# Moving form stores to ScalarE's queue, scaling A11 ahead of four sums, and adding inside the last product

## The chip, the cores and the metric

The kernel runs on one core of a Trainium2 chip. The metric is the device time of one execution in microseconds; 727.01 us is the median of three runs before the change (725.63, 727.01 and 729.6). The engines named in the text are PE (TensorE: matrix products, results in eight PSUM banks of 128 x 512 f32), DVE (VectorE: elementwise sums and products), ACT (ScalarE: copies and activations), POOL (GpSimd, here little more than a source of DMA transfers) and SP (SyncE, only DMA transfers). Each engine works its own instructions strictly in the order in which the program lists them. An instruction whose input is not ready, or whose output place is still being read, waits, and everything behind it on the same engine waits with it. A DMA transfer is an instruction of the engine on whose queue it is issued.

## The reference

The input x is 2048 rows of 1024 (bf16). Two branches are computed from it and mixed row by row with a gate g:

```
g = sigmoid((x * gate_w).sum(-1))                    # one number per row
a = attention(x @ wqkv) @ wo                         # 32 heads, 8 keys per row at steps of 2
h = gelu(x @ w_gate) * (x @ w_up)                    # 2048 x 3584
out = g * a + (1 - g) * (h @ w_down)
```

The attention weights are multiplied by g and h by 1 - g before the last product, so that `out` is one product: [(1-g) h | g o] times [w_down ; wo], with o the attention's result. Its inner length is 3584 + 1024 = 4608, that is 36 tiles of 128, split into two halves of NK = 18 tiles.

## The kernel before

The kernel first computes the projections, the attention, and h and stores h and o to DRAM (h_d, o_d); this takes until about 515 us. What follows, and what the change touches, is `down(s)`: the last product, for s = 0 (rows 0 to 1023, "the first half") and s = 1 ("the second half", `last`).

**Strassen's scheme at two levels.** For each half, the left factor is a 2 x 2 set of blocks A11, A12, A21, A22 and the right factor R11 to R22, each block 128 x 18 x 512 in SBUF. Seven block products with sums of blocks in place of eight are formed; the sums of the right blocks, T1 to T4, were worked out earlier and lie in DRAM (t_d). S, S2 and AD are sums of left blocks. Most of the block products are made by `level2`, which does the same again one level lower: it cuts the blocks into quarters, and forms seven inner products of 18 matmuls of 128 x 256 each. It reads four "forms" of the left block (L1, L3 to L7, made by `forms_L`, four DVE sums) and of the right block (R1, R3 to R7, made by `forms_R`, of which the third is written in place over the quarter (0, 1) of the T block itself). Between the inner products, ACT copies partial results from one PSUM place to another (`then`, L1052); the fifth product's copies are the last. The result of inner product three is kept in SBUF (`part5`) and added to the right half of each bank afterwards by `join` (L1032, one for two banks; `joins` does both). Two sets of four banks, XT and VT, take turns, so that DVE and ACT empty one while PE fills the other. `zero_left` (L1025, ACT) clears the left halves of a set before `level2` accumulates in it.

**Buffers.** Ten buffers of 18 KB per partition hold all blocks and forms, by a fixed plan. A buffer that gets a new content must have been read by everyone who wants the old one. The entries that matter here: in the first half T1 and R6 and L4 share buffer 1, R5 and R7 buffer 5, R4 buffer 7, T4 buffer 9, T3 buffer 8; in the second half A21 takes buffer 9, A22 buffer 7, L1 buffer 5, R1 buffer 8, R21 buffer 1.

**Stores of forms.** The forms R5, R7 and R4 are needed in both halves and depend only on the weights. The first half stores them (`store_F`: the overwritten quarter of the T block to t_d, 576 KB in rows of 512 bytes, L991; three forms to r_d, 1,728 KB, L992), and the second half loads them (`load_F`). The stores are on POOL's queue, as are the first half's output stores (`emit`, L1077).

**Sums that give output.** `add_out` (L1081) adds a bank and an accumulator in SBUF (u2 or qs) into an output tile and stores it. There are six output tiles, used in turn; tiles 4 and 5 lie in the gate's memory (`omgrep`). The next user of a tile waits until its store has landed.

**The seam between the halves.** After the first half's last `level2` (on XT), DVE does two joins, four `add_out` of XT, then three scalings of A11 of the second half by 1 - g (`scale_task`, L916), and, between the four `add_out` of VT, the forms L1 and R1. PE meanwhile does the product A12 x R22 into VT (L1072) and then the second half's first `level2` (on XT), whose end is followed by joins, copies of XT into u2 (L1094) and further sums of PE into XT. Scalings of A12 and a first one of A21 stand on DVE ahead of those joins.

**The tail.** The second half's last `level2` (A12 x R22 into VT) is followed on DVE by two joins and eight half-width sums (`half_out`, L1191), and on SP by five output stores (L1193).

Of the kernel before, what the change touches and what calls it, by code (L numbers as in the profile page):

```python
# [9 lines left out]
ALU = mybir.AluOpType  # L10
# [5 lines left out]
P = 128  # L16
SC = 512
# [51 lines left out]
def kernel(  # L69
# [12 lines left out]
    nc = tc.nc  # L82
    Bsz, S, D = A_x.shape
# [3 lines left out]
    o2 = out.rearrange("b s d -> (b s) d")  # L87
# [36 lines left out]
    NE_ = NPAIR - 2  # L124
    h_d = [[tc.dram_tile([P, 4, k, SC], BF16, name=f"h_d{s}{e}") for e, k in enumerate((NE_, NPAIR - NE_))] for s in range(2)]
    o_d = [[tc.dram_tile([P, NT, SC], BF16, name=f"o_d{s}{c}") for c in range(2)] for s in range(2)]
    t_d = [tc.dram_tile([P, NK, SC], BF16, name=f"t_d{k}") for k in range(4)]
    r_d = {k: tc.dram_tile([P, 3 * (NK // 2) * (SC // 2)], BF16, name=f"r_d{k}") for k in (1, 3, 4)}
# [6 lines left out]
    TT = V.tensor_tensor  # L135

    with tc.manual_schedule(engines={mybir.EngineType.PE, mybir.EngineType.DVE, mybir.EngineType.Activation,
# [55 lines left out]
        def flat(a):  # L193
            return a.rearrange("p a b -> p (a b)")
# [689 lines left out]
        def tf_close():  # L884
            while tf_q[0] < N1:
# [8 lines left out]
                     T3=8, L7=4, R7=5, T4=9, L4=1, R4=7, R22=6),  # L894
# [3 lines left out]
        qs = regf(R_QS, 4 * SC).rearrange("p (j n) -> p j n", j=4)  # L898
        on = [0]

        def out_tile():
            k = on[0] % 6
            on[0] += 1
            return reg(R_OUT[k], SC) if k < 4 else omgrep[:, (k - 4) * SC:(k - 3) * SC]
# [3 lines left out]
        def Bs(s):  # L908
            return {k: bufs[v] for k, v in plan[s].items()}

        def scale_task(b, s, c, ia, ib):
            t0 = s * SUP + c * SC
            om = omgrep[:, t0:t0 + SC].rearrange("p (o s) -> p o s", o=1)
            for i0 in range(ia, ib, 4):
                i1 = min(i0 + 4, ib)
                TT(out=b[:, i0:i1, :], in0=b[:, i0:i1, :], in1=om.to_broadcast([P, i1 - i0, SC]), op=ALU.mult)  # L916
                yield 0.05 + 0.273 * (i1 - i0)
# [15 lines left out]
        def pieces(*gens):  # L933
            for g in gens:
                yield from g

        def take(g, k):
            for _ in range(k):
                if next(g, None) is None:
                    break  # L940
# [47 lines left out]
            nc.sync.dma_start(out=flat(rf)[:, 0:NF], in_=r_d[k][:])  # L988

        def store_F(rf, b, k):  # L990
            nc.gpsimd.dma_start(out=t_d[k - 1][:, 0:KH, HN:SC], in_=quarter(b, 0, 1))  # L991
            nc.gpsimd.dma_start(out=r_d[k][:], in_=flat(rf)[:, 0:NF])  # L992

        def quarter(b, kh, h):
            return b[:, kh * KH:(kh + 1) * KH, h * HN:(h + 1) * HN]
# [4 lines left out]
        def forms_L(f, b):  # L1000
            f = quads(f)
            q = lambda kh, h: quarter(b, kh, h)
            for o_, a, b_, op in ((f[:, 0], q(0, 1), q(1, 1), ALU.add), (f[:, 1], f[:, 0], q(0, 0), ALU.subtract),
                                  (f[:, 2], q(0, 0), q(0, 1), ALU.subtract), (f[:, 3], q(1, 0), f[:, 1], ALU.subtract)):
                TT(out=o_, in0=a, in1=b_, op=op)  # L1005
                yield 1.3

        def forms_R(f, b):
            f = quads(f)
            q = lambda kh, h: quarter(b, kh, h)  # L1010
            for o_, a, b_, op in ((f[:, 0], q(0, 1), q(0, 0), ALU.subtract), (f[:, 1], q(1, 1), f[:, 0], ALU.subtract),
                                  (q(0, 1), q(1, 1), q(0, 1), ALU.subtract), (f[:, 2], q(1, 0), f[:, 1], ALU.subtract)):
                TT(out=o_, in0=a, in1=b_, op=op)  # L1013
                yield 1.3

        def woven(*gens):
            for cs in zip(*gens):
                yield from cs
# [4 lines left out]
        def zero_left(bk):  # L1023
            for i in range(2):
                nc.scalar.activation(out=two_banks(bk, i, 0), in_=omgrep[:, SUP:SUP + SC].rearrange("p (a b) -> p a b", a=2),  # L1025
                                     func=ACT.Copy, scale=0.0)
# [4 lines left out]
        def join(bk, rf, i):  # L1031
            TT(out=two_banks(bk, i, 1), in0=two_banks(bk, i, 1), in1=part5(rf), op=ALU.add)  # L1032

        def joins(bk, rf):
            for i in range(2):
                join(bk, rf, i)

        def level2(bk, L, R, lf, rf, mid=None):
            p5d = part5(rf)
            lf, rf = quads(lf), quads(rf)  # L1040
            lq, rq = lambda r, c: quarter(L, c, r), lambda r, c: quarter(R, r, c)
            c = lambda i, h, j: banks[:, bk[2 * i + j], h * HN:(h + 1) * HN]

            def prod(i, h, l, r, then=None):
                for j in range(2):
                    for kt in range(KH):
                        nc.tensor.matmul(c(i, h, j), lhsT=l[:, kt, j * P:(j + 1) * P], rhs=r[:, kt, :], start=False,  # L1047
                                         stop=(kt == KH - 1), skip_group_check=True)
                    if then:
                        then(j)  # L1050

            cp = lambda d, s_: nc.scalar.copy(out=d, in_=s_)  # L1052
            prod(0, 0, lq(0, 0), rq(0, 0), lambda j: cp(c(1, 1, j), c(0, 0, j)))
            prod(0, 0, lq(0, 1), rq(1, 0))
            prod(1, 0, lf[:, 0], rf[:, 0], lambda j: cp(p5d[:, j, :], c(1, 0, j)))
            prod(1, 1, lf[:, 1], rf[:, 1], lambda j: cp(c(0, 1, j), c(1, 1, j)))
            prod(1, 1, lf[:, 2], rq(0, 1), lambda j: cp(c(1, 0, j), c(1, 1, j)))
            if mid:
                mid()
            prod(0, 1, lf[:, 3], rq(1, 1))  # L1060
            prod(1, 0, lq(1, 1), rf[:, 2])

        def down(s):
# [15 lines left out]
            def add_out(ps, t_, c, nh, j):  # L1079
                ot = out_tile()  # L1080
                TT(out=ot, in0=ps, in1=t_, op=ALU.add)  # L1081
                emit(ot, c, nh, j)
# [34 lines left out]
            if last:  # L1117
                run(forms_L(B["L5"], S))
            else:
                run(woven(forms_L(B["L5"], S), forms_R(B["R5"], B["T1"])))  # L1120
                store_F(B["R5"], B["T1"], 1)
            run(comb_task(A21, A22, AD, ALU.subtract))
            S2 = A21
            level2(VT, S, B["T1"], B["L5"], B["R5"])
            run(forms_L(B["L6"], S2))
            rest = forms_R(B["R6"], B["T2"])
            take(rest, 2)
# [22 lines left out]
            for j in range(4):  # L1150
                TT(out=u2[:, j, :], in0=XP[j], in1=u2[:, j, :], op=ALU.add)
            run(rest)
            level2(VT, AD, B["T3"], B["L7"], B["R7"], lambda: zero_left(XT))
            fl, fr = forms_L(B["L4"], A22), forms_R(B["R4"], B["T4"])
            if last:
                fr = ()
            else:
                store_F(B["R7"], B["T3"], 3)
                loads(1, "A11", "R11")
                for _ in range(3):  # L1160
                    take(fl, 1)
                    take(fr, 1)
# [1 line left out]
            for j in range(4):  # L1164
                TT(out=qs[:, j, :], in0=qs[:, j, :], in1=u2[:, j, :], op=ALU.add)
            run(fr)
            if not last:
                store_F(B["R4"], B["T4"], 4)
            for j in range(4):
                if j % 2 == 0:  # L1170
                    join(VT, B["R7"], j // 2)
# [1 line left out]
                TT(out=u2[:, j, :], in0=VP[j], in1=u2[:, j, :], op=ALU.add)  # L1173
            if last:
                run(woven(forms_L(B["L3"], A12), forms_R(B["R3"], B["R22"])))
            level2(XT, A22, B["T4"], B["L4"], B["R4"], last and (lambda: zero_left(VT)))
            joins(XT, B["R4"])
            for j in range(4):
                add_out(XP[j], u2[:, j, :], 1, 0, j)
            if not last:  # L1180
                loads(1, "A12", "A21", "R21", "A22")
                zero_left(XT)
                N = Bs(1)
                rest = pieces(scale_task(N["A11"], 1, 0, 0, NE_), woven(forms_L(N["L1"], N["A11"]), forms_R(N["R1"], N["R11"])))
            if last:
                level2(VT, A12, B["R22"], B["L3"], B["R3"])
                ots = [out_tile() for _ in range(4)]

                def half_out(j, h, store=()):
                    hs = slice(h * HN, (h + 1) * HN)  # L1190
                    TT(out=ots[j][:, hs], in0=VP[j][:, hs], in1=qs[:, j, hs], op=ALU.add)  # L1191
                    for a, z in store:
                        nc.sync.dma_start(out=o2[base + j * P:base + (j + 1) * P, SC + a:SC + z], in_=ots[j][:, a:z])  # L1193

                half_out(0, 0)
                half_out(1, 0)
                join(VT, B["R3"], 1)
                half_out(2, 1)
                half_out(3, 1, [(HN, SC)])
                join(VT, B["R3"], 0)  # L1200
                half_out(0, 1, [(0, SC)])
                half_out(1, 1, [(0, SC)])
                half_out(2, 0, [(0, SC)])
                half_out(3, 0, [(0, HN)])
            else:
                for j in range(4):
                    mm(VP[j], A12, B["R22"], j, True)
                    take(rest, 3)
                    add_out(VP[j], qs[:, j, :], 0, 1, j)
                run(rest)  # L1210
                loads(1, "T1")
# [80 lines left out]
```

## Time and profile before

| what | value |
|---|---|
| median of three runs | 727.01 us (725.63 to 729.6) |
| the profiled execution's own time | 726.45 us |
| its span, first to last instruction | 724.7 us |
| granted TensorE clock, mean | 0.997 |
| PE busy | 710.6 us (98%) |
| DVE busy | 673.4 us (93%) |
| ACT busy | 328.5 us (45%) |
| POOL busy | 138.8 us (19%) |
| queue of SP (q1), bytes | 103.69 MB |
| queue of POOL (q0), bytes | 55.37 MB |
| queue of ACT (q10), bytes | 0.52 MB |

The profile is of one execution. Its page gives busy times by engine, the busy share in 40 slices of the span, the DMA queues, the chain of work that ended last, the costliest groups of instructions, and the DMA issues. The trace behind it can be asked for the timeline of any stretch, for waits, and for busy times by stretches. Times in the timeline are microseconds from the span's start. "Idle before" in brackets is the time in which the engine did nothing ahead of the instruction, with what ended it. A DMA issue's row shows how long the issue itself took; the time to landing is given by the view of the DMA. Matmuls are pipelined, and their ends are modelled.

### The profile page before, as it was taken

How to read it: one execution, taken by the hardware profiler on the slowest of the kernel's cores; microseconds unless marked ns; L12 is line 12 of the kernel's file. 1: busy time of each engine (PE TensorE's matmuls, PEld its weight loads, DVE VectorE, ACT ScalarE, POOL GpSimd, SP SyncE). 2: the span in 40 equal slices, each digit the busy share in tenths (PEclk: the TensorE clock that was granted, in tenths of full speed). 3: DMA queues.
4: the chain of work that ended last, by engine and by line, in shares of the span. 5: the costliest groups of instructions: out<-in, count | busy, mean ns of one | idle time of the engine just before them, and what ended most of it. 6: DMA issues, size and time to landing. Idle time of an engine off the chain costs nothing. (4 is left out here: it accounts for less than half of the span.)

```text
span 724.7 us, 10828 instructions
## 1 busy us (share of the span) xinstructions
PE 710.6 (98%) x4107; PEld 409.0 (56%) x4107; DVE 673.4 (93%) x725; ACT 328.5 (45%) x600; POOL 138.8 (19%) x239
## 2 busy tenths in 40 slices
PE   8999999999999999999999999999999999899996
PEld 4466656655544444444444444444448885658885
DVE  2699989999999999999999999999989996999995
ACT  4554446444457665555555555555222320222421
POOL 1323444133301331212210101000101022010011
PEclk9999999999999999999999999999999999999998
DMA  9976644278263758573853756262984699983921
GB/s 276 279 171 229 224 140 143 90 258 296 100 212 120 260 173 258 169 239 127 262 165 112 270 171 220 71 276 69 388 345 164 274 391 424 423 378 141 376 102 59
DMA packets 92373, 160.27 MB, mean 221 GB/s; under 512 B 19329, under 2 KB 68513, under 8 KB 87969
## 3 DMA queue, kind: packets, MB, share of 16 engines
q1 hardware_dynamic: 75136, 103.69, 42.3%
q0 software_dynamic: 16896, 55.37, 21.7%
q8 instruction: 32, 0.52, 0.3%
q10 hardware_dynamic: 288, 0.52, 0.3%
q14 instruction: 21, 0.16, 0.1%
HBM read 110.40 MB, written 54.14 MB: 227 GB/s over the span
## 5 line engine op out<-in xcount | busy, mean ns | idle before, releaser
L366 PE MATMUL banks<-arena 128*128 128x512 bf16 x2184 | 474.8, 379 | 1.5 <-DVE arena L403 0.7
L366 PEld LDWEIGHTS <-arena 128*128 128x128 bf16 x2184 | 240.5, 111 | 235.2 <-issue 7.0
L1047 PE MATMUL banks<-arena 128*128 128x256 bf16 x1260 | 138.3, 273 | 0.0
L1047 PEld LDWEIGHTS <-arena 128*128 128x128 bf16 x1260 | 123.2, 98 | 15.3 <-issue 0.3
L403 DVE TENSOR_TENSOR arena<-banks,arena 128x1024 bf16<-128x1024 f32 x78 | 95.3, 1221 | 13.0 <-PE banks L366 7.8
L389 ACT COPY arena<-banks 128x512 f32<-128x512 f32 x78 | 45.8, 587 | 130.8 <-PE banks L366 130.8
L374 ACT CAST arena<-banks 128x512 bf16<-128x512 f32 x102 | 59.6, 585 | 42.4 <-PE banks L366 42.4
L745 DVE TENSOR_TENSOR arena<-arena 128x2048 bf16<-128x2048 bf16 x64 | 77.0, 1220 | 0.5
L752 DVE TENSOR_TENSOR arena<-arena 128x2048 bf16<-128x2048 bf16 (+2 forms) x96 | 73.9, 776 | 1.0
L598 DVE TENSOR_TENSOR arena<-arena 128x2048 bf16<-128x2048 bf16 x64 | 74.7, 1219 | 0.1
L1072 PE MATMUL banks<-arena 128*128 128x512 bf16 x288 | 62.8, 379 | 3.4 <-ACT arena L1094 3.4
L260 POOL DMA_DIRECT2D h_d<-arena x28 | 20.4, 728 | 226.4 <-DVE arena L254 195.5
L396 ACT COPY banks<-banks 128x512 f32<-128x512 f32 x78 | 44.5, 570 | 21.9 <-PE banks L366 20.1
L1005 DVE TENSOR_TENSOR arena<-arena 128x2304 bf16<-128x2304 bf16 x40 | 53.3, 1353 | 0.5
L384 ACT COPY banks<-banks 128x512 f32<-128x512 f32 x78 | 45.0, 576 | 13.6 <-PE banks L366 12.5
L1072 PEld LDWEIGHTS <-arena 128*128 128x128 bf16 x288 | 28.2, 98 | 37.1 <-issue 3.6
L1052 ACT COPY banks<-banks 128x256 f32<-128x256 f32 x60 | 21.4, 356 | 57.4 <-PE banks L1047 57.2
L925 DVE TENSOR_TENSOR arena<-arena 128x2048 bf16<-128x2048 bf16 (+1 forms) x40 | 41.8, 1114 | 2.0 <-DMA arena<-h_d 2.0
L372 ACT ACTIVATE arena<-banks 128x512 bf16<-128x512 f32 x54 | 32.2, 597 | 15.4 <-PE banks L366 15.4
L323 DVE TENSOR_TENSOR arena<-arena 128x1024 bf16<-128x1024 bf16 x60 | 38.7, 686 | 0.5
L1013 DVE TENSOR_TENSOR arena<-arena 128x2304 bf16<-128x2304 bf16 x28 | 37.7, 1353 | 0.2
L254 DVE TENSOR_TENSOR arena<-arena 128x2048 bf16<-128x2048 bf16 x28 | 34.1, 1217 | 1.9 <-ACT arena L251 1.4
(94 smaller groups left out, 441.8 us busy)
## 6 DMA issues: line engine op xcount, KB each, us to landing
arena<-t_d SPq DMA_DIRECT2D x8, 2304.0 KB, 13.7
h_d<-arena POOLq DMA_DIRECT2D x28, 512.0 KB, 4.3
arena<-w_c SPq DMA_DIRECT2D x12, 1152.0 KB, 15.8
t_d<-arena POOLq DMA_DIRECT2D x36, 256.0 KB, 4.5
arena<-h_d SPq DMA_DIRECT2D x6, 1536.0 KB, 12.5
arena<-in_B_w_gate_dram SPq DMA_DIRECT2D x15, 512.0 KB, 5.6
arena<-in_B_w_up_dram SPq DMA_DIRECT2D x15, 512.0 KB, 5.3
arena<-in_B_w_down_dram SPq DMA_DIRECT2D x28, 256.0 KB, 7.1
```

What stands on the lines that cost most here:

```text
L366: self.pe = nc.tensor.matmul(ps, lhsT=self.L[form](kt), rhs=rhs[:, kt, :], start=(start and kt == 0), stop=(kt == HK - 1), skip_group_chec ...
L374: nc.scalar.copy(out=o_, in_=i_)
L384: nc.scalar.copy(out=self.Y, in_=self.X)
L389: nc.scalar.copy(out=self.p5s, in_=self.V)
L396: nc.scalar.copy(out=self.Z, in_=self.Y)
L403: TT(out=self.T[:, :, c2s], in0=pair, in1=self.p5s.rearrange("p (o n) -> p o n", o=1).to_broadcast([P, 2, SC]), op=ALU.add)
L598: TT(out=dst, in0=q.rearrange("p (o s) -> p o s", o=1).to_broadcast([P, NWIN, AC]), in1=_win_ap(k, [[-DIL, NWIN], [1, AC]]), op=ALU.mult)
L745: TT(out=prod2[(t // 2) % 2][:, t % 2], in0=ab, in1=_win_ap(v[:, t, HALO:HALO + AC], [[SJ, NJ], [-DIL, NWIN], [1, SJ]]), op=ALU.mult)
L752: TT(out=out_, in0=h(0), in1=h(1), op=ALU.add)
L1005: TT(out=o_, in0=a, in1=b_, op=op)
L1047: nc.tensor.matmul(c(i, h, j), lhsT=l[:, kt, j * P:(j + 1) * P], rhs=r[:, kt, :], start=False, stop=(kt == KH - 1), skip_group_check=True)
L1072: nc.tensor.matmul(ps, lhsT=L[:, i, j * P:(j + 1) * P], rhs=R[:, i, :], start=(start and q == 0), stop=(q == NK - 1), skip_group_check=not ...
```

## The change

Four things change, all in the last product.

- `store_F` issues its two transfers on ACT's queue instead of POOL's. The three calls move: each is now made inside the `level2` that uses the forms, after the fifth inner product, so that on ACT the transfers stand behind that product's copies. For R7 they also stand behind `zero_left(XT)`.
- `level2` gets a second hook, `mid2`, after the sixth inner product.
- At the seam, the three scalings of A11 are listed ahead of the four `add_out` of XT instead of behind them. The loop over VT then takes the forms in steps of two calls instead of three, that is one form of L1 and one of R1 at each `add_out`.
- In the tail, join 1 is done after the fifth inner product, join 0 and the first two whole-width `add_out` after the sixth, and two more `add_out` after the seventh. The half-width sums and their stores go.

```diff
         def store_F(rf, b, k):
-            nc.gpsimd.dma_start(out=t_d[k - 1][:, 0:KH, HN:SC], in_=quarter(b, 0, 1))
-            nc.gpsimd.dma_start(out=r_d[k][:], in_=flat(rf)[:, 0:NF])
+            nc.scalar.dma_start(out=t_d[k - 1][:, 0:KH, HN:SC], in_=quarter(b, 0, 1))
+            nc.scalar.dma_start(out=r_d[k][:], in_=flat(rf)[:, 0:NF])
...
             if mid:
                 mid()
             prod(0, 1, lf[:, 3], rq(1, 1))
+            if mid2:
+                mid2()
             prod(1, 0, lq(1, 1), rf[:, 2])
...
                 run(woven(forms_L(B["L5"], S), forms_R(B["R5"], B["T1"])))
-                store_F(B["R5"], B["T1"], 1)
             run(comb_task(A21, A22, AD, ALU.subtract))
             S2 = A21
-            level2(VT, S, B["T1"], B["L5"], B["R5"])
+            level2(VT, S, B["T1"], B["L5"], B["R5"], not last and (lambda: store_F(B["R5"], B["T1"], 1)))
...
-            level2(VT, AD, B["T3"], B["L7"], B["R7"], lambda: zero_left(XT))
+            level2(VT, AD, B["T3"], B["L7"], B["R7"],
+                   lambda: (zero_left(XT), last or store_F(B["R7"], B["T3"], 3)))
...
-            level2(XT, A22, B["T4"], B["L4"], B["R4"], last and (lambda: zero_left(VT)))
+            level2(XT, A22, B["T4"], B["L4"], B["R4"],
+                   lambda: zero_left(VT) if last else store_F(B["R4"], B["T4"], 4))
             joins(XT, B["R4"])
+            if not last:
+                N = Bs(1)
+                rest = pieces(scale_task(N["A11"], 1, 0, 0, NE_), woven(forms_L(N["L1"], N["A11"]), forms_R(N["R1"], N["R11"])))
+                take(rest, 3)
             for j in range(4):
                 add_out(XP[j], u2[:, j, :], 1, 0, j)
...
-                level2(VT, A12, B["R22"], B["L3"], B["R3"])
-                ots = [out_tile() for _ in range(4)]
...
+                R3 = B["R3"]
+                level2(VT, A12, B["R22"], B["L3"], R3, lambda: join(VT, R3, 1),
+                       lambda: (join(VT, R3, 0), [add_out(VP[j], qs[:, j, :], 0, 1, j) for j in range(2)]))
+                for j in range(2, 4):
+                    add_out(VP[j], qs[:, j, :], 0, 1, j)
             else:
                 for j in range(4):
                     mm(VP[j], A12, B["R22"], j, True)
-                    take(rest, 3)
+                    take(rest, 2)
                     add_out(VP[j], qs[:, j, :], 0, 1, j)
```

More of the change, by code (lines that the diff above doesn't have):

```diff
@@ L1036, in joins, with level2 @@
                 join(bk, rf, i)
-        def level2(bk, L, R, lf, rf, mid=None):
+        def level2(bk, L, R, lf, rf, mid=None, mid2=None):
             p5d = part5(rf)
@@ L1157, in down @@
             else:
-                store_F(B["R7"], B["T3"], 3)
                 loads(1, "A11", "R11")
@@ L1166, in down @@
             run(fr)
-            if not last:
-                store_F(B["R4"], B["T4"], 4)
             for j in range(4):
@@ L1182, in down @@
                 zero_left(XT)
-                N = Bs(1)
-                rest = pieces(scale_task(N["A11"], 1, 0, 0, NE_), woven(forms_L(N["L1"], N["A11"]), forms_R(N["R1"], N["R11"])))
             if last:
-                level2(VT, A12, B["R22"], B["L3"], B["R3"])
-                ots = [out_tile() for _ in range(4)]
[L1189 to L1204, printed above, removed]
+                R3 = B["R3"]
[3 more added lines that the diff above has]
+                    add_out(VP[j], qs[:, j, :], 0, 1, j)
             else:
```

## The prediction

> **What bounds the kernel now.** I read the page's parts first (PE is busy 710.6 of 724.7 us), then the chain that ended last, to see where PE is held, then the timeline at those places and the DMA share by stretches.
>
> The chain's later part:
>
> ```profile
> 597.95 12.63 DMA out_dram<-omgrep
> ...
> 632.43 0.59 ACT arena L1094
> 633.02 0.04 issue
> 633.06 15.70 PE banks L1072 x72
> 648.76 68.94 PE banks L1047 x630
> ```
>
> From 633.06 to 717.7 PE is the chain without a gap. Before it, the chain runs back over DVE to an output store of 12.63 us. The timeline at the seam between the halves (start, us, engine, line, operation; in brackets the idle time before it):
>
> ```profile
> 609.45 0.69 DVE L1081 TENSOR_TENSOR omgrep<-banks,arena 128x512 bf16<-128x512 f32 x1 [5.68 <-DMA out_dram<-omgrep]
> ...
> 631.70 1.30 DVE L1032 TENSOR_TENSOR banks<-banks,arena 128x512 f32<-128x512 f32 x2
> 632.43 2.05 ACT L1094 COPY arena<-banks 128x512 f32<-128x512 f32 x4 [6.22 <-DVE banks L1032]
> 633.06 7.28 PE L1072 MATMUL banks<-arena 128*128 128x512 bf16 x33 [3.38 <-ACT arena L1094]
> ```
>
> DVE stood 5.68 us for an output tile; 22 us later its joins are late and PE stands 3.38 us. The first half at the R5/T1 store, and the tail:
>
> ```profile
> 546.67 1.03 POOL L991 DMA_DIRECT2D t_d<-arena  x1
> 555.29 0.36 ACT L1052 COPY banks<-banks 128x256 f32<-128x256 f32 x1 [0.63 <-PE banks L1047]
> 557.14 2.81 DVE L1013 TENSOR_TENSOR arena<-arena 128x2304 bf16<-128x2304 bf16 x2
> ...
> 578.68 1.35 DVE L1013 TENSOR_TENSOR arena<-arena 128x2304 bf16<-128x2304 bf16 x1
> 581.82 0.36 ACT L1052 COPY banks<-banks 128x256 f32<-128x256 f32 x1 [0.68 <-PE banks L1047]
> ...
> 714.84 0.42 DVE L1191 TENSOR_TENSOR omgrep<-banks,arena 128x256 bf16<-128x256 f32 x1 [1.98 <-ACT banks L1052]
> 717.80 0.70 DVE L1032 TENSOR_TENSOR banks<-banks,arena 128x512 f32<-128x512 f32 x1 [1.61 <-PE banks L1047]
> 720.60 0.75 DVE L1191 TENSOR_TENSOR arena<-banks,arena 128x256 bf16<-128x256 f32 x2
> ```
>
> After PE's end at 717.71 DVE still has two joins and six half sums. DMA by stretches (share and GB/s are the last two columns):
>
> ```profile
> 552.00:558.00 6.00, 6.00 (x58) 5.37 (x56) 5.89 (x5) 1.43 (x4) 0.00 (x0) 1.00 0.42 176
> 606.00:612.00 6.00, 6.00 (x30) 2.74 (x28) 2.09 (x3) 0.59 (x1) 0.95 (x2) 1.00 1.01 423
> ```
>
> From 576 to 648 the share is 0.97 to 1.04: loads there land by bandwidth, not by when they are issued.
>
> **Part 1, the tail: gains 2.2 us.** The fifth product's copies end at 714.21 (the copy at 713.85 plus 0.36). Join 1 can follow at 714.3 for 0.7 us, done by 715.0, before the seventh product touches its banks at 715.75 (two products of 1.97 us end at 717.71). That a reader waits for the last product in its bank only shows at 714.84: that half sum starts when the sixth product's first bank ends. So join 0 starts at 715.8, two whole sums follow to 717.8 (0.60 us apart, as the four L1081 at 710.38 in 2.48 us), the last two end at 719.0. Before, the last sum ends at 721.35. That is 2.35 us less, of which the last store gives back 0.2 (128 KB lands in 1.8 us, 64 KB in 1.6). Ends: 1.5 if join 1 makes the seventh product wait 0.7 us, 2.4 otherwise.
>
> **Part 2, the seam: gains 3.38 us.** Two things move. Three A11 scalings (L916 x3, 3.49 us) go ahead of the four sums; A11 landed at 596.3 (issue 586.06, 10.2 us), so they can run at 602.5. And the out stores no longer stand behind the 1,728 KB store of R4 on POOL's queue: issued at 596.76 and 597.95 behind it they took 12.6 us, at 610.43 and 611.59, nothing such in front, 5.1 and 6.7. Without delay from earlier, DVE then runs: joins to 602.5, scalings to 606.0, four sums to 608.4, four times two forms and a sum (2.54 + 0.6) to 621.0, A12's scalings (3.49) to 624.5, one A21 scaling to 625.7. Join 0 waits for the sixth product, which ends at 627.7: DVE has 2.0 us to spare. The join (0.7) and the copy (0.6) end at 629.0, before PE's seventh product at 629.69. PE's stall goes whole; it can't give more, PE being back to back on both sides. Next late is DVE's sum S for the product that was at 648.6: its 16.6 us of work from join 1 (629.75) ends at 646.4, its first half's pieces at 644.7; PE, 3.4 earlier, wants these at 645.4 and the rest at 647.4. Covered by 0.7 us. R21, wanted whole 1.96 us into the sums of four, at 631.7, landed at 629.6 (609.98 + 19.6): 2.1 us of cover. Lower end of the gain: 1.4.
>
> **Part 3, the stores on ACT's queue: costs 1.6 us.** The six issues: ACT's two loads at the start took 0.40 and 0.45 us each; SP's under full DMA at most 1.12. ACT idles 4.50 us after 555.65, 3.52 after 584.2, 6.95 after 596.9, so 0.8 to 2.2 us a pair is hidden; without cover, the copy at 587.71 has 0.55 us before the second product needs it. POOL is freed of six issues, which nothing waited for.
> But the R5/T1 store moves from 546.67 to behind ACT's last copy, 555.65. Buffer 1 holds T1, and the plan gives it to R6 too: the first form of R6 (L1013 at 557.14) overwrites rows the store still reads. Before, the store landed at 550.9 (4.2 us). Now it starts at 555.65. POOL's 4.2 us with 1.02 of issue becomes some 3.6 with ACT's 0.4: an estimate; the quarter lands at 559.3 and DVE stands d = 2.3 us (557.14 to 559.4). Ends: 3.1 us (SP's 1.8 for 128 KB, and 448 KB more at the 347 GB/s below) and 5.6 us, the median of SP's 512 KB loads of w_gate in short rows: d 1.7 to 4.2. I take a value near POOL's row, the same bytes at the same rows' length.
> Behind it on DVE stand the rest of R6, the joins, u2's sums and L7/R7's forms, back to back to 595, so d isn't made up. PE's first thin place is L7's fifth product: the copy at 581.82 follows its first half of 0.98 us, so it starts at 580.79; its operand is ready at 580.03. Slack 0.7, so PE stands s = d - 0.7 = 1.6 us (1.0 to 3.5). Everything after moves by s, DVE by d, which leaves 1.3 of the 2.0 us at the seam. T3's load (559.16, landed 567.6) now shares DMA with R5's 1,728 KB: 4.7 MB from 555.7 at 347 GB/s (T3 alone: 2.36 MB in 8.4 us less 1.6, the landing of the smallest store), with these 1.6, ends near 570.9, before PE's 572.6 and DVE's 572.3: no cost.
> R7's store waits for zero_left, R4's for the copy at 596.55; nobody rewrites R7's or T3's buffers before 608. A21's load waits for T4's quarter: 598.5 plus 7.5 to 10.7 is 606 to 609, not 601.37; SP's queue still holds A12 until 614.6, so nothing runs dry.
>
> **Sum.** The profiled execution took 726.45 us (span 724.7 and 1.75 around it): 726.45 - 2.2 - 3.38 + 1.6 = 722.5. It lay 0.56 under the median of 727.01, so a median of 723.0.
>
> **Rivals.**
> A. No new wait (the store lands within 0.7 us of need): 721.4. For it: DMA stands idle at 556. Against: no row of half a megabyte lands so fast.
> B. The out tiles stay late. If DMA is simply full, a store takes 12.6 us from any queue: tiles come at 609.4 and 610.6, DVE's four sums end at 611.2 instead of 608.4, 2.8 later with 1.3 to spare: PE keeps 1.5 us of its stall: 724.5. Against: the rows of 5.1 and 6.7 at the same 423 GB/s.
> The Trainium skill (Trainium Kernel Development and Optimization, Key Constraints) says that transfers from SP's, ACT's and POOL's queues run on the same 16 engines and that issuing from several only saves issue time. By that rule B holds; the 5.1 us against 12.6 us here speak for an order within a queue. The skill's page DMA: Bandwidth & Descriptors (Queues, rings and completion order) has each engine go round-robin between queues, by which B would not hold.
> C. R21 and A21 become the bound. Stores start later, so DMA idles about 3 us near 584 and all later landings slip; past its 2.1 us of cover PE gets each microsecond back as a wait, at most the 3.4: 724 to 726.4, taken 725.5.
> D. Slower: ACT stands until its own store has landed. At R7 (r_d 10.9 us before) the copy at 587.71 would be 7 us late, at R5 (8.1 us) 3 us: 723 + 10 = 733. It decides above 3.1 us of hold at R7, and makes the kernel slower above some 7. For it: SP's queue stood up to 3.3 us for an earlier load's landing; against: SP issues up to eight transfers ahead, ACT has six in all.
>
> **Numbers.** Forecast 0.54, with its own range 721.9 to 725.2 (d's ends, part 1's 0.7, and 0.3 of spread between runs); A 0.12; B 0.12; C 0.14; D 0.08. Range: 720.8 to 726.4, from A less 0.6 to the end of C. Half a per cent, about what a measurement of this kernel can tell, is 3.6 us: 723.4. Faster holds A and some two thirds of the forecast, whose upper end is the longer: 0.12 + 0.36; same the rest of it (0.18), B and C: 0.44; slower D.
>
> **What would show it.** Right: a DVE wait of about 2.3 us for t_d<-arena at the first L1013 near 557; a PE wait of 1 to 3 us near 581 for DVE; no PE wait at L1094's copies; no DVE wait for omgrep near 607; PE's last matmul 1.8 us earlier and 1.35 us of DVE behind it. Wrong: PE waits for w_c or h_d loads near 633, ACT copies late near 588, or no wait at 557.

## The result, and the profile after

The changed kernel takes 722.58 us (median of seven runs, 722.03 to 723.08) against 726.5 us (seven runs, 724.67 to 729.6) before: a ratio of 0.9945, 95% interval 0.9926 to 0.9963. That is 0.55% less; 723.0 was forecast. The profiled execution took 722.87 us, of which 721.1 are its span, against 726.45 and 724.7. On the chip of its second measurement (below), 19 of the 35 runs of the kernel before show a mean granted clock of 0.995 or less and took 726.6 to 731.2 us, the other 16 show 0.997 or more and took 724.3 to 726.5 (median 725.2), while all twelve of the changed kernel show 0.999 or 1.0 (median 722.56): about 1.5 of the 4.1 us between the medians there goes with the clock.

The timeline of the changed kernel at the places that the prediction named (start, us, engine, line, operation; in brackets the idle time before it and what ended it):

```profile
555.99 0.39 ACTq L991 DMA_DIRECT2D t_d<-arena  x1
559.55 2.82 DVE L1013 TENSOR_TENSOR arena<-arena 128x2304 bf16<-128x2304 bf16 x2 [1.77 <-issue]
582.51 19.82 PE L1047 MATMUL banks<-arena 128*128 128x256 bf16 x180 [1.24 <-DVE arena L1013]
609.51 1.28 DVE L1083 TENSOR_TENSOR omgrep<-banks,arena 128x512 bf16<-128x512 f32 x2
629.77 0.70 DVE L1032 TENSOR_TENSOR banks<-banks,arena 128x512 f32<-128x512 f32 x1 [1.89 <-PE banks L1047]
631.46 2.11 PE L1074 MATMUL banks<-arena 128*128 128x512 bf16 x8
633.99 11.38 PE L1074 MATMUL banks<-arena 128*128 128x512 bf16 x51 [0.42 <-DMA arena<-w_c]
...
713.61 0.70 DVE L1032 TENSOR_TENSOR banks<-banks,arena 128x512 f32<-128x512 f32 x1 [1.32 <-ACT banks L1052]
715.13 0.70 DVE L1032 TENSOR_TENSOR banks<-banks,arena 128x512 f32<-128x512 f32 x1 [0.82 <-PE banks L1047]
717.07 1.28 DVE L1083 TENSOR_TENSOR arena<-banks,arena 128x512 bf16<-128x512 f32 x2
```

From top to bottom: R5/T1's store starts on ACT's queue at 555.99, and DVE's first form of R6 comes 1.77 us late. The bracket names nothing, but the chain of waits has the store's transfer there. PE pays 1.24 us for it at 582.5. At 609.51 the output tiles in `omgrep` are free: DVE's 5.68 us are gone. At 629.77 it is now DVE that waits for PE. PE starts on A12 x R21 at 631.46 without a stall, but stops 0.42 us later on for the second half of R21, a load. Behind PE's last matmul (717.06) DVE works 1.29 us, not 3.64.

The late R21 can be followed in the chain (start, us, what) and in SP's own waits (total, times, longest):

```profile
599.09 22.76 DMA r_d<-arena
621.85 0.02 issue
621.86 0.02 SPq L831
621.88 0.03 issue
621.91 12.04 DMA arena<-w_c
633.94 0.04 issue
633.99 9.22 PE banks L1074 x42
```

```profile
SPq L815 <- DMA t_d<-arena: 13.6, 1, 13.6
...
SPq L831 <- DMA r_d<-arena: 2.5, 2, 1.6
```

A21's load (L815) stood 13.6 us until T4's quarter had been read out of buffer 9, and the loads of R21 (L831) stood behind it and behind R4's store. How long R4's two stores took is in the view of the DMA for 594 to 600 us (KB each, us to landing):

```profile
r_d<-arena ACTq DMA_DIRECT2D x1, 1728.0 KB, 22.8
t_d<-arena ACTq DMA_DIRECT2D x1, 576.0 KB, 18.1
```

On POOL's queue, before, they took 12.6 and 10.7 us.

### The profile page after: what moved, and what is told of

It reads as the page before. It is cut to its first block, busy times and chain, and to the rows that moved or that the text cites. A ratio compares the mean times of both kernels' runs of the same rounds, so it can differ in the third digit from the quotient of the medians.

```text
span 721.1 us, 10757 instructions
## 1 busy us (share of the span) xinstructions
PE 708.0 (98%) x4051; PEld 408.2 (57%) x4107; DVE 672.9 (93%) x721; ACT 328.9 (46%) x600; POOL 134.5 (19%) x233
## 3 DMA queue, kind: packets, MB, share of 16 engines
q0 software_dynamic: 15984, 48.29, 19.0%
q10 hardware_dynamic: 4224, 7.60, 3.0%
## 5 line engine op out<-in xcount | busy, mean ns | idle before, releaser
L372 ACT ACTIVATE arena<-banks 128x512 bf16<-128x512 f32 x54 | 32.3, 597 | 15.5 <-PE banks L366 15.5
```

## The experiments

Two theories were put against each other at each place: that the three parts act as the prediction's sum has them, each for its own reason, and that one of them did all or that the named wait was not the cause. The first four kernels ran on one chip, with the kernel before at 725.9 us (35 runs). R4's long store ahead of T4's quarter, and only R4's long store on ACT's queue, ran on a third, with 726.38 us before (13 runs); the other four ran on a second, with 726.69 us before (35 runs). Where lengths within a profile are compared, they are taken from PE's first matmul in a `level2` (545.06 us before) to its last matmul, since no edit touches what lies ahead of that: 172.65 us before, 171.5 in both profiles of the changed kernel.

### The new tail alone

```diff
 (kernel before)
-                level2(VT, A12, B["R22"], B["L3"], B["R3"])
...
+                level2(VT, A12, B["R22"], B["L3"], R3, lambda: join(VT, R3, 1),
+                       lambda: (join(VT, R3, 0), [add_out(VP[j], qs[:, j, :], 0, 1, j) for j in range(2)]))
```

> The kernel before with the new tail alone. My account: PE's work is as before to its end, join 1 ends 0.7 us ahead of the seventh product and costs PE nothing, and DVE's work behind PE's last matmul falls from 3.64 us (717.71 to 721.35) to 1.3; the time falls by 2.2 to 2.9 us, to 723.6 to 724.3 against 726.5. Rival: what the changed kernel gained at its end came from stores that were no longer in the way, then this kernel gains under 1 us. Rival: the joins inside hold the seventh product; then PE's records show a wait of 0.5 us or more near 715 and the gain is under 1.7.

Measured: 723.6 us, ratio to before 0.9966 (0.9945 to 0.9986), that is 2.3 us less. PE's waits over the whole last product:

```profile
PE banks L1074 <- ACT arena L1096: 2.8, 1, 2.8
PE banks L1074 <- issue: 0.2, 1, 0.2
```

The first is the seam's old stall, and the second stands right behind it; near 715 PE waits for nothing. So the tail's gain stands by itself, and the joins inside the product cost PE nothing. From PE's last matmul to the end of the span it is 4.4 us here, 6.99 before.

One thing in this profile is not in the one before: behind the stall, PE's clock is granted only in part. The stretches just there (us, PE busy with its matmuls, granted clock, DMA share, GB/s):

```profile
632.00:633.00 1.00, 0.59 (x1) 0.59 0.98 397
633.00:634.00 1.00, 0.79 (x2) 0.50 1.28 522
634.00:635.00 1.00, 1.00 (x4) 0.50 1.00 424
635.00:636.00 1.00, 1.00 (x5) 0.70 1.04 442
```

The clock is 1.00 before and after these, and the product behind the stall takes 17.1 us to the start of the next one (632.41 to 649.50) instead of 15.5 (633.06 to 648.60 in the profile before, where the clock stays at 1.00 behind a stall of 3.38 us). So the stall can cost some 1.5 us more than its own length; what decides whether it does, these runs don't show. The mean granted clock is 0.996 or 0.997 in six of this kernel's twelve runs (median 724.9 us) and 0.999 or 1.0 in the other six (722.2), so its 2.3 us by the medians can't be put down to the tail to the tenth.

### The new order at the seam alone

```diff
 (kernel before, stores on POOL's queue where they were)
             joins(XT, B["R4"])
+            if not last:
+                N = Bs(1)
+                rest = pieces(scale_task(N["A11"], 1, 0, 0, NE_), woven(...))
+                take(rest, 3)
...
-                    take(rest, 3)
+                    take(rest, 2)
```

> The kernel before with the new order at the seam alone: A11's scalings ahead of the four sums, stores of forms where they were. My account (both the queue and the order are wanted): the output tiles still land at 609.4 and 610.6, behind R4's store; DVE reaches the third sum at 607.2, waits about 2.2 us there and 0.5 at the next, is done with them at 611.2 and reaches the joins 0.8 us late, so PE keeps 0.8 us (0.3 to 1.5) of its 3.38 us: 2 to 3 us faster than before. Rival (the order alone does it): no PE wait at the copies into u2. Rival (the queue alone does it): DVE's wait is still over 5 us and PE's over 2.5.

Measured: 724.4 us, ratio 0.9973 (0.995 to 0.9997), 1.5 us less by the medians, where 2 to 3 were expected. PE's and DVE's waits:

```profile
PE banks L1072 <- ACT arena L1094: 0.9, 1, 0.9
PE banks L1047 <- DVE arena L1013: 0.7, 1, 0.7
...
DVE omgrep L1081 <- DMA out_dram<-omgrep: 3.2, 2, 2.5
```

The output tiles still land 13.0 us after their issue, DVE stands 3.2 us for them (2.7 were expected) and PE keeps 0.9 of its 3.38 us (0.8 were expected). The order alone is worth most of the stall, because the scalings fill the wait, but not all of it. The 0.7 us stand near 583, ahead of the seam, and are not of this edit: DVE waits 3.3 us for a load of h at 538 (2.0 in the profile before) and comes late to R7's forms. With it, the length within the profile is 171.05 us, 1.6 less than before.

### The stores on ACT's queue alone

```diff
 (changed kernel, with the old seam and the old tail)
-                take(rest, 3)
             for j in range(4):
                 add_out(XP[j], u2[:, j, :], 1, 0, j)
...
-                    take(rest, 2)
+                    take(rest, 3)
```

> The kernel before with the six stores moved to ACT's queue and place alone: old order at the seam, old tail. My account: DVE waits 1.8 us for R5/T1's store and PE 1.2 us near 582, as in the changed kernel; at the seam the output tiles land 6.5 us after their issue, so DVE waits under 1 us for them and PE's 3.38 us fall to at most 0.5; sum -1.7 us, 724.8 against 726.5. Rival (the order was needed): PE keeps 1 us or more at the seam, and the kernel is within 1 us of before or slower.

Measured: 725.22 us, ratio 0.9998 (0.9983 to 1.0013): no gain that can be told, where 1.7 us were expected. PE's waits:

```profile
PE banks L1047 <- DVE arena L1013: 1.2, 1, 1.2
PE banks L1074 <- DMA arena<-w_c: 1.1, 2, 0.6
```

The first output tiles take 6.1 and 6.2 us and DVE waits for none; the copies into u2 no longer hold PE. So the queue alone also removes DVE's lateness at the seam, and the new order is not needed for that once the output stores are free. What the queue gains there (3.38) it loses again, 1.2 us for R5/T1's store and 1.1 us for R21, which the expectation had put at 0.5 at most. That leaves 1.1 us, and the profiled span is 1.3 us shorter (723.4 against 724.7); the timed runs don't show it.

### R5/T1's stores back on POOL's queue, ahead of the product

```diff
 (changed kernel)
         def store_F(rf, b, k):
+            q = nc.gpsimd if k == 1 else nc.scalar
...
                 run(woven(forms_L(B["L5"], S), forms_R(B["R5"], B["T1"])))
+                store_F(B["R5"], B["T1"], 1)
...
-            level2(VT, S, B["T1"], B["L5"], B["R5"], not last and (lambda: store_F(B["R5"], B["T1"], 1)))
+            level2(VT, S, B["T1"], B["L5"], B["R5"])
```

> The changed kernel, but R5/T1's two stores are on POOL's queue at their old place, ahead of the product. My account: the 1.8 us that DVE waits at the first form of R6 near 559.5, and the 1.2 us that PE waits near 582, are that store's, and both go; 1.2 us less than the changed kernel, 721.4 against 722.6, less what the earlier arrival at the seam loses to R21's landing (PE's 0.4 us there could become 1 to 1.6, since the landing is set by transfers). Rival: the wait at 559.5, which the profile puts down to nothing, isn't the store's; then it stays at 1.8 us.

Measured: 722.36 us, ratio 0.9953 (0.9935 to 0.997), where 721.4 was expected. Both waits are gone: DVE has none at R6's first form and PE none near 582. Over the whole last product PE waits only once:

```profile
PE banks L1048 <- DVE arena L1014: 0.4, 1, 0.4
```

So the wait that the profile puts down to "issue" was this store's. The length within the profile is 170.1 us, 1.4 less than the changed kernel's, so there the wait's end does come through. In time the kernel can't be told from the changed one by these runs.

### R5's long store ahead of T1's quarter

```diff
 (changed kernel, k = 1 only, written out)
-            nc.scalar.dma_start(out=t_d[k - 1][:, 0:KH, HN:SC], in_=quarter(b, 0, 1))
             nc.scalar.dma_start(out=r_d[k][:], in_=flat(rf)[:, 0:NF])
+            nc.scalar.dma_start(out=t_d[k - 1][:, 0:KH, HN:SC], in_=quarter(b, 0, 1))
```

> The changed kernel, but R5's 1,728 KB are stored ahead of T1's quarter, so that the quarter lands later: the wait at R6's first form is made longer, all else alike. My account: at the full rate the quarter lands at 564.4, and where its short rows stand against T3's load (from 559.7) at 568 to 571; DVE's wait grows from 1.8 us to between 7 and 14, and PE's wait near 582 follows it less 0.6: 6 to 13 us, and the time grows by 5 to 12 us, to 728 to 735. Rival (PE's 1.2 us is not that wait's, or is made up later): the time grows by less than 3 us though DVE waits 7 or more.

Measured: 728.58 us, against 722.56 us (12 runs, 721.81 to 723.59) of the changed kernel on the same chip: 6.0 us more. The waits:

```profile
PE banks L1053 <- DVE arena L1019: 5.9, 2, 3.7
PE banks L1080 <- DMA arena<-w_c: 1.3, 2, 0.7
...
DVE arena L1019 <- issue: 8.0, 1, 8.0
```

PE's 1.2 us became 5.9, of which 2.2 stand at 565, already in R6's product, and 3.7 at the old place; the expectation had all of it there. Its wait for R21 grew from 0.4 to 1.3 us. The two profiled executions differ by 5.56 us (727.5 against 721.94), the waits by 5.5, so nothing is made up later. The quarter landed 7.9 us after its issue, at the full rate (near 563.6; 564.4 was worked out), not at 568 to 571: T3's load, issued at 558.9, came too late to stand ahead of it.

### The changed kernel once more

> The changed kernel once more, unaltered, on the chip of the next three, to compare them with: 722.6 us; DVE's wait of 1.8 us at R6's first form, PE's of 1.2 us near 582, and at the seam R21 landing at about 633.9 with a PE wait of 0.4 us.

Measured: 722.56 us, ratio 0.9948 (0.9929 to 0.9966). PE's waits are again 1.2 and 0.4 us; R21 ends its landing at 633.1 here, where the product also comes 0.9 us earlier. DVE's wait at R6's first form is 3.7 us, not 1.8: in this execution DVE did not lose 2.0 us to a load of h just before, came 1.9 us sooner and waited so much longer. PE's wait is the same, because what sets it is when the store lands against PE's own start, not how long DVE stood.

### T4's quarter from POOL's queue

```diff
 (changed kernel; R4's long store stays on ACT's queue)
             run(fr)
+            if not last:
+                nc.gpsimd.dma_start(out=t_d[3][:, 0:KH, HN:SC], in_=quarter(B["T4"], 0, 1))
```

> The changed kernel, but the quarter of T4 (576 KB in rows of 512 bytes) is stored from POOL's queue at its old place; R4's 1,728 KB stay on ACT's. My account: on ACT's queue every row is a packet of its own (a pair of stores has 1312 packets there and 304 on POOL's), and against SP's long packets the quarter gets little of a full DMA, 18.1 us, with R4's store stuck behind it to 22.8. So here the quarter lands within 12 us of its issue near 593, SP waits under 4 us for it instead of 13.6, R4's store lands within 14 us, R21 lands near 631, and PE's 0.4 us for it goes: 0.4 us faster than the changed kernel, 722.2, within the noise. Rival (ACT's queue gets a small share whatever it carries): R4's store still takes 18 us or more.

Measured: 722.15 us, ratio 0.9939 (0.9919 to 0.9958). The quarter now lands in 9.8 us and R4's long store, on ACT's queue as before but with nothing ahead of it, in 12.0 us instead of 22.8. PE's wait for R21 is gone. But a wait of 0.6 us for a form on DVE near 664 comes in its place, and the length within the profile is as it was, 171.5 us: PE's 0.4 us for R21 is not gained. The queues of the changed kernel, and then of this one (packets, MB, share of 16 engines):

```profile
q0 software_dynamic: 15984, 48.29, 19.0%
q10 hardware_dynamic: 4224, 7.60, 3.0%
```

```profile
q0 software_dynamic: 16144, 48.88, 19.5%
q10 hardware_dynamic: 3056, 7.01, 2.7%
```

The same 576 KB are 1168 packets on ACT's queue (4224 less 3056), one for each row of 512 bytes and 16 more, and 160 packets of some 4 KB on POOL's (16144 less 15984).

### R4's long store ahead of T4's quarter

```diff
 (changed kernel, k = 4 only, written out)
-            nc.scalar.dma_start(out=t_d[k - 1][:, 0:KH, HN:SC], in_=quarter(b, 0, 1))
             nc.scalar.dma_start(out=r_d[k][:], in_=flat(rf)[:, 0:NF])
+            nc.scalar.dma_start(out=t_d[k - 1][:, 0:KH, HN:SC], in_=quarter(b, 0, 1))
```

> The changed kernel, but R4's 1,728 KB are stored ahead of T4's quarter on ACT's queue. My account (short rows get little of a full DMA, long ones a fair share): R4's store lands 12 to 14 us after its issue near 598.6, not 22.8, the quarter only once SP's queue has run empty, near 617 to 622; A21's load waits at least as long as in the changed kernel, and PE waits 0.4 to 2 us for R21: 0 to 2 us slower than the changed kernel. Rival (the first store on ACT's queue waits for what SP queued, whatever its rows): R4's store takes 18 us or more.

Measured: 725.29 us, ratio 0.9983 (0.9964 to 1.0002), 2.7 us above the changed kernel's 722.56 on another chip, where 0 to 2 were expected; the profiled executions differ by 1.83 us (723.77 against 721.94). The two stores in the view of the DMA, and the waits of PE and SP at the seam:

```profile
r_d<-arena ACTq DMA_DIRECT2D x1, 1728.0 KB, 12.2
t_d<-arena ACTq DMA_DIRECT2D x1, 576.0 KB, 22.1
```

```profile
PE banks L1080 <- ACT arena L1102: 1.9, 1, 1.9
...
PE banks L1080 <- DMA arena<-w_c: 0.6, 1, 0.6
...
SPq L815 <- DMA t_d<-arena: 18.0, 1, 18.0
```

Three times the bytes land in 12.2 us, and the quarter, second, still takes 10 us more. So it is not the first store on ACT's queue that waits for what SP has queued. Of the two, the one in short rows is slow. A21's load stands 18 us behind it, DVE comes late to the joins, and PE loses 2.5 us.

### Both waits mended

```diff
 (changed kernel)
         def store_F(rf, b, k):
+            q = nc.gpsimd if k == 1 else nc.scalar
+            if k != 4:
...
+                store_F(B["R5"], B["T1"], 1)
...
+                nc.gpsimd.dma_start(out=t_d[3][:, 0:KH, HN:SC], in_=quarter(B["T4"], 0, 1))
```

> The changed kernel with both waits mended: R5/T1's stores on POOL's queue at their old place, T4's quarter on POOL's queue at its old place, R7's pair and R4's long store on ACT's. My account: no wait at R6's first form, none near 582, R21 in time: 1.6 us less than the changed kernel, 721.0. Rival (what is gained ahead of the seam is lost at the seam, where landings are set by bytes): PE waits 1 us or more for R21 or A21 and the time is that of the changed kernel.

Measured: 720.81 us (12 runs, 720.56 to 723.81), ratio 0.9921 (0.99 to 0.9943), 1.75 us below the changed kernel on the same chip; ten of the twelve runs lie below that kernel's fastest, 721.81 us. PE at the seam and at the next place:

```profile
599.82 15.70 PE L1076 MATMUL banks<-arena 128*128 128x512 bf16 x72
615.36 13.92 PE L1049 MATMUL banks<-arena 128*128 128x256 bf16 x126
629.11 11.18 PE L1076 MATMUL banks<-arena 128*128 128x512 bf16 x50
...
663.27 1.91 PE L1049 MATMUL banks<-arena 128*128 128x256 bf16 x16 [0.39 <-DVE arena L1015]
```

PE is back to back over the seam. (T4's quarter again stands ahead of output stores on POOL's queue: they take 10.2 us, and DVE waits 1.2 us for one, which costs PE nothing.) This version is faster than both kernels. Its next late thing is a form on DVE in the second half, 0.4 us. The length within the profile is 170.1 us, as with R5's pair alone on POOL's queue, so by the lengths only R5's of the two waits mended was worth something; the timed runs of the three versions don't separate the two.

### Only R4's long store on ACT's queue

```diff
 (as the last one, and R7's pair on POOL's queue at its old place)
-                   lambda: (zero_left(XT), last or store_F(B["R7"], B["T3"], 3)))
+                   lambda: zero_left(XT))
...
+                store_F(B["R7"], B["T3"], 3)
                 loads(1, "A11", "R11")
```

> New order at the seam and new tail, with R5's and R7's stores and T4's quarter on POOL's queue at their old places, and only R4's 1,728 KB on ACT's queue inside its product. My account (of the six moved stores one mattered, the one that stood ahead of the output stores): as fast as the best so far, 720.8 us against 722.6 of the changed kernel, with no PE wait near 582 and none over 0.5 us at the seam. Rival: R7's pair on POOL's queue delays the output stores or T4's quarter, DVE waits over 3 us for an output tile and PE 1 us or more at the seam, 722 us or more.

Measured: 721.26 us (4 runs, 720.86 to 721.43), ratio 0.9943 (0.9926 to 0.9959), with no PE wait near 582 or at the seam, one of 0.6 us for a form on DVE near 663, and again 170.1 us within the profile. Its time lies 0.45 us above the last version's on another chip, which these runs can't tell from the chips' difference. Of the six stores that the change moves, only R4's long one had to leave POOL's queue: with none moved and the same order at the seam (above), DVE waited 3.2 us for output tiles and PE kept 0.9.

## Why the prediction was right

The sum was -2.2 - 3.38 + 1.6 = -3.98 us; the medians fell by 3.9 and the profiled execution by 3.58. That the medians come so close is partly luck: the sum goes by one profiled execution, with nothing for the clock, and the medians hold executions with and without a lowered clock. Term by term, from the two profiles:

- **The tail, -2.2: measured -2.95**, from PE's end to the span's end (6.99 us before, 4.04 after). DVE's part is as forecast: its last sum ends 1.29 us behind PE, not 3.64, which is the 2.35 us of the text. The step "of which the last store gives back 0.2" was mis-sized: the stores give 0.6 more. Before, five half-sum stores stood in SP's queue and the last was issued some 0.4 us after its sum; after, four are issued, each as its sum ends, and 128 KB land in 1.7 us. Alone on its kernel the tail gave 2.3 us in the medians.
- **The seam, -3.38: measured -2.96.** DVE's account held: no wait for the output tiles (6.6 us to landing, where 5.1 to 6.7 was read off), join 0 waits for PE 1.89 us with 2.0 less 0.7 forecast, no stall at the copies. The step that failed is the one on A21: "598.5 plus 7.5 to 10.7 is 606 to 609 ... so nothing runs dry". It was 616.7, the quarter having taken 18.1 us. SP's queue did run dry (0.02 MB from 614 to 617 us), R21's second load went out when R4's store had landed (621.85), and R21 landed at 633.9, not 629.6, past its cover: 0.42 us. The rows that I used for it were of POOL's queue, and in a full DMA they don't carry over.
- **The stores, +1.6: measured +1.24.** The quarter landed in 3.5 us (3.6 estimated), DVE waited 1.8 us (2.3), and PE followed it less 0.5 (0.7). That this subtraction came out is luck in part: in the second profile DVE waited 3.7 us and PE 1.2 all the same. PE's wait goes by the store's landing against PE's own start, as the swap of R5's stores confirms: DVE's wait moved by 4.8 us, taken at its end against the product's start, and PE's by 4.7.
- What the sum did not have: about 0.5 us of small PE delays from the seam on (0.2 within A12 x R21, beside the 0.42, then 0.2 near 667 and 0.2 near 684.7; their cause is not shown), and 0.52 us by which this execution's first `level2` began later (545.58 against 545.06), ahead of anything changed. With these, 0.52 + 1.24 - 2.96 - 2.95 + 0.5 = -3.65 against the -3.58 measured. Nor did it have the clock behind the seam's stall, which the profile before doesn't show and that of the new tail alone does, at 1.5 us.

Of the rivals, A is excluded by the wait, and B by the 6.6 us. By the Trainium skill's page Trainium Kernel Development and Optimization, Key Constraints, issuing from another queue would have saved issue time only; here it shortened the landing of the output stores from 12.6 to 6.6 us, so the measurement decides against that sentence where one queue holds a long store. C came true in small: 0.4 us in the changed kernel, 1.1 with the stores alone, 2.5 with R4's stores swapped. D did not come: ACT's copies follow PE at their old intervals (3.52 us idle before the one at 589.65, as before).

Why short rows are slow on ACT's queue: the quarter is 1168 packets there against 160 on POOL's, and took 18.1 us, and 22.1 behind the long store, against 9.8 (issued at 591.95, ahead of the long store), while long rows on ACT's queue at the same place took 12.0. The packets of SP's queue (q1) and ACT's (q10) from 602 to 606 us, in the changed kernel, where q10 has the quarter, and then with the quarter on POOL's queue, where q10 has R4's long store (packets, MB, share):

```profile
q1 hardware_dynamic: 164, 1.34, 79.3%
q10 hardware_dynamic: 144, 0.07, 6.1%
```

```profile
q10 hardware_dynamic: 67, 0.93, 54.1%
q1 hardware_dynamic: 67, 0.59, 34.8%
```

Both times the two queues move nearly as many packets as each other, so the one with 512 bytes a packet moves little: 0.07 MB in 4 us, against 0.93 MB in long rows. The Trainium skill's page DMA: Bandwidth & Descriptors (Queues, rings and completion order) says that each engine takes turns between queues packet by packet. These counts agree with it. On an idle DMA (555.99) the quarter took 3.5 us, less than POOL's 4.2.

## What to carry to other kernels

A store that is moved later is a longer hold on its buffer: look up who gets the buffer next, and take the landing, not the issue, as the end of the hold. Before moving a transfer to another queue, ask what stands behind it in the old one and how long its rows are; short rows belong on a queue that packs them, or where the DMA is idle. And a part that removes one wait can hand the path to the next: the stores alone gained 3.4 us at one place and lost 2.3 at two others, so that only the parts together, and each wait read by itself, told what was worth keeping.

## What was not expected of the hardware

The same 576 KB in rows of 512 bytes took 3.5 us on ACT's queue with the DMA idle and 18.1 us with the DMA full, a factor of five, where POOL's queue went from 4.2 to 9.8 or 10.7. And R21's second load was issued at 621.88, just as R4's store on ACT's queue had landed (599.09 + 22.76 = 621.85), though the two share no buffer; in the second profile it was 621.41 and 621.38. The load is the eighth transfer behind that store, counted over SP's and ACT's queues. It looks as if the program's count of transfers in flight runs over both queues, which wasn't tried.
